# phi written as exp(min(x, 0)) + max(x, 0): two ScalarE reads of the PSUM bank, a sum on GpSimd, shared staging tiles and a new order

## The chip, the core and the metric

The kernel runs on one core of one Trainium2 chip, in one launch. The time is device microseconds of that core. The kernel before took 338.68 us as the median of three runs (338.31 to 340.45). A profiled execution of it, from which all durations below come, took 337.45 us.

## The reference

Two independent results are computed and set side by side. The first is a memory-augmented attention over 2048 positions of 448 features: 16 heads of 28 features, 4 segments of 512 positions. The second is a state-space convolution of another 2048x448 input.

```python
phi = lambda t: jnp.where(t > 0, t + 1.0, jnp.exp(t))
for s in range(N):                       # 4 segments
    qs, ks, vs = q[:, :, s], k[:, :, s], v[:, :, s]
    logits = einsum("bhqd,bhkd->bhqk", qs, ks) * scale + mask
    a_dot = einsum("bhqk,bhkd->bhqd", softmax(logits), vs)
    pq = phi(qs)
    num = einsum("bhld,bhde->bhle", pq, M)
    den = einsum("bhld,bhd->bhl", pq, z)[..., None] + 1e-6
    outs.append(g * num / den + (1.0 - g) * a_dot)
    pk = phi(ks)
    M = M + einsum("bhld,bhle->bhde", pk, vs)
    z = z + einsum("bhld->bhd", pk)
return concat(outs) @ wo                 # and, beside it, y + u * D_skip
```

For the second result the kernel has a short form, a running sum along the positions, that it uses where a bound computed on the chip allows it. For these inputs the running sum is what the chip executes; the general convolution is skipped.

## The kernel before, in words

**Tiling.** The 16 heads are taken four at a time, 32 partitions to a head (28 features, the others carry sums and the softmax maximum). A unit of work t = 4s + g is one group g of four heads in one segment s; t runs from 0 to 15. For each unit there are these stages, each a function of the kernel:

- `P_proj` (lines 470, 474, 475): q and k of the unit, 11 matmuls each into one PSUM bank; ScalarE writes the high half and VectorE the low half of each value, so that products keep float32 accuracy.
- `phi` (lines 495 to 497): phi of q or of k, from the same PSUM bank, or, for the k of group 3, from a sum of the halves in SBUF.
- `M_upd` (522, 524, 530, 538, 540): phi(k) is transposed, copied to SBUF by ScalarE, multiplied with v and added to the memory M.
- `P_num` (508, 510): phi(q) times M.
- `Q1` (558, 566): logits row block by row block in three parts. Each part fills four banks, one a head; VectorE reduces each bank to a row maximum (a custom instruction and a read of its accumulator). `Q1_max` (573 to 577) transposes the maxima and sends them by DMA into the rows of q.
- `Q2` (593, 597, 600): transposed logits with the maximum subtracted, again in three parts of four banks; ScalarE takes the exponential of each bank into P0, P1 or P2 and GpSimd blanks the upper triangle.
- `PV` (617) multiplies with v; the row sums travel by DMA (`rc`), are inverted on VectorE and spread into buffers `R` (632 to 639).
- `C_unit` (683 to 690): GpSimd multiplies by `R`, adds the two parts and takes the low half; `C_last` does the same for t = 15 mostly on VectorE, in two halves of the positions.
- `V_tile` (428, 431) makes v, `W_tile` (701, 707) the output projection, four parts (one for each group) of three matmuls to a tile.
- `B_tile` (761 to 770): a tile of the convolution; ScalarE scales into `sc`, VectorE scans (764), GpSimd carries the last column and adds (766, 769).

**PSUM.** There are eight banks, and all stages draw from the same eight (room "f"). A part of `Q1` or `Q2` takes four of them at once.

**Three tilings of the array.** `Q1` and `Q2` put the four heads in four strips of rows of the array, `PV` and the second half of `M_upd` in four strips of columns, and all other matmuls use the whole array. They are called row, column and full below.

**Order.** Every operation is first recorded in a list by `Plan.op`, with its engine and the tiles that it reads and writes. `Plan.write` then emits the operations one after the other in the order of the table ORDER. So the table alone decides where an instruction stands in the queue of its engine, and which buffer of a room it gets: the one that has been free longest at that place. Each engine works through its queue in that order; an instruction that waits for a buffer or an operand holds up all that stand behind it on its engine. SyncE issues most of the DMAs, in the order of its own queue. The priorities in AT are recorded with the operations, but do not take part in the emission.

The tiles that the change touches are declared in these lines:

```python
room("R", 2, [P, 512], F32)
room("u", 2, [112, 512], F32)
room("sc", 1, [112, 512], F32)
```

Of the kernel before, what the change touches and what calls it, by code (L numbers as in the profile page):

```python
# [8 lines left out]
F32 = mybir.dt.float32  # L9
F32R = mybir.dt.float32r  # L10
I32 = mybir.dt.int32
AF = mybir.ActivationFunctionType
# [6 lines left out]
P = 128  # L19
# [236 lines left out]
def attn_s4d_kernel(tc, xT, wq, wk, wv, wo, beta, u, uT, lar, aim, crl, cim, ldt, dsk, ldc, dsc, oa, yT):  # L256
# [5 lines left out]
    with ExitStack() as ctx:  # L262
# [23 lines left out]
        room("P1", 2, [P, 4, 384], F32)  # L286
        room("P2", 1, [P, 4, 384], F32)
        room("pvn", 2, [P, 2, 512], F32)
        room("R", 2, [P, 512], F32)
        room("oh", 5, [P, 512], F32R)  # L290
        room("ol", 5, [P, 512], F32R)
        room("u", 2, [112, 512], F32)
# [609 lines left out]
```

## Time and profile before

| | |
|---|---|
| median of three runs | 338.68 us |
| profiled execution | 337.45 us, of it the span from first to last instruction 335.5 us and 1.95 us around it |
| TensorE (PE) | 319.9 us busy, 95% of the span |
| VectorE (DVE) | 246.4 us, 73% |
| ScalarE (ACT) | 215.0 us, 64% |
| GpSimd (POOL) | 163.3 us, 49% |
| chain that ended last | PE 83%, DVE 6%, ACT 5%, DMA 3%, issue 2% |

How to read it: the busy time of PE says that it nearly always has a matmul under way, but a matmul that waits for its operands or its bank, or that runs at a lowered clock, also counts as under way. The chain is the better guide to what sets the end: it follows back, from the last instruction, to whatever released each step. The time that it gives to DVE, ACT, DMA or issue is time in which PE was held up. The row PEclk of the page, and the column PEclk of a table by stretches, give the share of the TensorE clock that was granted. In the profile, `L566` and the like are lines of the kernel; buffer numbers are left out of the names.

### The profile page before, as it was taken

The page shows a single profiled execution, that of the slowest core. Times are in us where ns is not written, and L with a number is a line of the kernel's source. Part 1 is how long each engine was busy: PE and PEld are TensorE (multiplying, and loading weights), DVE is VectorE, ACT ScalarE, POOL GpSimd, SP SyncE. Part 2 cuts the span into 40 slices and gives each one's busy share as a digit, 9 for nine tenths or more (in the row PEclk, how much of TensorE's full clock was granted, in tenths as well). Part 3 has the DMA queues.
Part 4 walks back from the last instruction along what each step waited for, and adds up shares of the span by engine and source line. Part 5 has one row for each costly group of instructions (what it writes and reads, how often), then busy time and mean ns, then how long its engine had stood idle before and what let it go on. Part 6 is the DMA issues. An engine that isn't in the chain of part 4 may idle for free.

```text
span 335.5 us, 8677 instructions
## 1 busy us (share of the span) xinstructions
PE 319.9 (95%) x3221; PEld 220.2 (66%) x3221; DVE 246.4 (73%) x777; ACT 215.0 (64%) x439; POOL 163.3 (49%) x208
## 2 busy tenths in 40 slices
PE   7999989998999999999999999899999999899992
PEld 2677866686686577677767777666666757546662
DVE  2999986798869794954899846677498868446680
ACT  4845378986794659778845865558743565757721
POOL 9035046346281628555654412587471361746920
PEclk9999989999999999999999969999999999979999
DMA  7942232211221203121022310310100131110113
GB/s 211 308 141 68 78 116 91 69 59 59 74 63 43 78 31 109 55 71 42 6 82 96 93 65 24 95 59 4 39 8 4 37 110 40 41 53 10 57 55 113
DMA packets 16584, 23.92 MB, mean 71 GB/s; under 512 B 4364, under 2 KB 9500, under 8 KB 16540
## 3 DMA queue, kind: packets, MB, share of 16 engines
q1 hardware_dynamic: 16252, 22.82, 22.0%
q10 hardware_dynamic: 288, 0.52, 0.6%
q8 instruction: 26, 0.43, 0.6%
q14 instruction: 18, 0.15, 0.2%
HBM read 13.64 MB, written 7.36 MB: 63 GB/s over the span
## 4 chain that ended last, share of the span: by engine, by line
PE 83%; DVE 6%; ACT 5%; DMA 3%; issue 2%; ACTq 0%; DVEq 0%
PE f L470 22%; PE f L558 13%; PE f L701 11%; PE f L617 11%; PE f L593 10%; PE f L428 10%; PE f L508 3%; ACT P L597 3%; DVE f L566 2%; DMA P<-in_wk 2%; PE f L522 2%; PE f L530 1%; DMA rc<-pvn 1%; PE f L573 1%; DVE mx L566 1%
## 5 line engine op out<-in xcount | busy, mean ns | idle before, releaser
L566 DVE CUSTOM_DVE_ANT_0 f<-f,mask 128x384 f32<-128x384 f32 (+3 forms) x256 | 118.0, 521 | 31.9 <-PE f L558 27.1
L597 ACT ACTIVATE P<-f 128x384 f32<-128x384 f32 (+1 forms) x192 | 89.3, 536 | 18.3 <-PE f L593 17.3
L600 POOL TENSOR_SCALAR_AFFINE_SELECT P<-P 128x512 f32<-128x512 f32 x64 | 41.5, 666 | 48.7 <-ACT P L597 48.6
L558 PE MATMUL f<-k,q 28*128 28x384 f32 (+3 forms) x768 | 51.6, 353 | 3.3 <-DMA q<-mr 1.4
L593 PE MATMUL f<-q,k 29*128 29x256 f32 (+3 forms) x768 | 48.2, 346 | 1.5 <-DVE mx L566 0.6
L683 POOL TENSOR_TENSOR pvn<-pvn,R 128x512 f32<-128x512 f32 x26 | 34.6, 1338 | 30.8 <-DVE R L639 24.7
L558 PEld LDWEIGHTS f<-k,q 28*128 28x128 f32 x768 | 32.5, 188 | 21.3 <-DVE mx L566 7.1
L593 PEld LDWEIGHTS f<-q,k 29*128 29x128 f32 x768 | 32.6, 190 | 15.8 <-ACT P L597 4.7
L617 PE MATMUL f<-P,vb 128*32 128x256 f32 (+3 forms) x528 | 39.7, 440 | 0.0
L566 DVE DVE_READ_ACCUMULATOR2_ANT mx<- 128x1 f32 x256 | 35.9, 140 | 0.1
L617 PEld LDWEIGHTS f<-P,vb 128*32 128x32 f32 x528 | 17.3, 112 | 21.3 <-issue 16.0
L690 POOL TENSOR_TENSOR ol<-pvn,oh 128x512 fp32r<-128x512 f32 x15 | 19.3, 1284 | 19.4 <-ACT oh L689 19.4
L470 PE MATMUL f<-xh,wh_q 128*128 128x512 f32 x64 | 28.3, 443 | 0.0
L701 PE MATMUL f<-wh_o,oh 128*128 128x448 f32 x64 | 26.6, 415 | 0.8 <-ACT oh L673 0.7
L764 DVE TENSOR_TENSOR_SCAN sc<-ones,carry,sc 112x512 f32<-112x512 f32 x16 | 23.0, 1435 | 5.0 <-ACT sc L762 4.9
L470 PE MATMUL f<-xh,wl_q 128*128 128x512 f32 x64 | 25.9, 405 | 0.0
L428 PE MATMUL f<-wh_v,xh 128*128 128x448 f32 x64 | 25.4, 397 | 0.0
L769 POOL TENSOR_TENSOR u<-u,sc 112x512 f32<-112x512 f32 x16 | 20.5, 1283 | 7.7 <-ACT u L767 7.7
L428 PE MATMUL f<-wl_v,xh 128*128 128x448 f32 x64 | 23.4, 365 | 0.0
L701 PE MATMUL f<-wl_o,oh 128*128 128x448 f32 x64 | 23.4, 365 | 0.0
L701 PE MATMUL f<-wh_o,ol 128*128 128x448 f32 x64 | 23.4, 365 | 0.0
L470 PE MATMUL f<-xh,wh_k 128*128 128x512 f32 x48 | 21.1, 441 | 1.9 <-ACT xin L524 1.1
(138 smaller groups left out, 568.7 us busy)
## 6 DMA issues: line engine op xcount, KB each, us to landing
u<-in_uT SPq DMA_DIRECT2D x16, 224.0 KB
out_y<-u SPq DMA_DIRECT2D x16, 224.0 KB
out_a<-os SPq DMA_DIRECT2D x16, 224.0 KB
xin<-in_xT SPq DMA_DIRECT2D x12, 256.0 KB
P<-in_xT SPq DMA_DIRECT2D x4, 256.0 KB
k<-q SPq DMA_DIRECT2D x64, 16.0 KB
P<-in_wv SPq DMA_DIRECT2D x4, 224.0 KB
xin<-in_wo SPq DMA_DIRECT2D x4, 224.0 KB
```

Source lines behind the costliest of these rows:

```text
L428: nc.tensor.matmul(pv.ap, X(s, x, c).ap[:, cs], (wl if w else wh).ap[:, c], start=a, stop=b)
L470: nc.tensor.matmul(pp.ap, (wl if w else wh).ap[:, g, c], X(s, x, c).ap, start=a, stop=b)
L558: nc.tensor.matmul(bank[h].ap[:, c0:c0 + n], q.ap[rows(h), qb, a, :], k.ap[rows(h), 0:qb + 1, b, :], start=(i == 0), stop=(i == 2))
L566: nc.vector.tensor_tensor_reduce(sc, sc, mask[:, 512 - n:512], 1.0, -3.0e38, ALU.add, ALU.max, mx.ap[:, 4 * h + qb:4 * h + qb + 1])
L593: nc.tensor.matmul(bank[h].ap[:, c0:c0 + w], k.ap[rows(h, 29), kb, a, :], q.ap[rows(h, 29), kb:4, b, :], start=(i == 0), stop=(i == 2))
L597: Q.op("ACT", act(n), pri + 0.01 * h, lambda h=h: nc.scalar.activation(pb.ap[:, h, 0:n], bank[h].ap[:, 0:n], AF.Exp, scale=SCALE), r=[bank ...
L600: Q.op("POOL", 700, pri + 0.1, lambda c0=c0: nc.gpsimd.affine_select(pb.ap[:, :, c0:c0 + P], pb.ap[:, :, c0:c0 + P], [[0, 4], [1, P]], ALU ...
L617: nc.tensor.matmul(pvp.ap[32 * h:32 * h + 32, q0:hi], VB(s, kb).ap[:, 4 * g + h, :], pb.ap[:, h, c0 + q0 - kb * P:c0 + hi - kb * P], start ...
L683: nc.gpsimd.tensor_tensor(pvn.ap[:, i, :], pvn.ap[:, i, :], R[i].ap, ALU.mult)
L701: nc.tensor.matmul(po.ap, o.ap[:, cs], w.ap[:, g], start=(g == 0 and i == 0), stop=(g == 3 and i == 2))
L764: Q.op("DVE", 1354, pri, lambda: nc.vector.tensor_tensor_scan(sc.ap, ones.to_broadcast([112, 512]), sc.ap, cj, ALU.mult, ALU.add), r=[sc, ...
L769: Q.op("POOL", 1344, pri, lambda: nc.gpsimd.tensor_tensor(ut.ap, ut.ap, sc.ap, ALU.add), r=[ut, sc], w=[ut])
```

## The change

The value of phi is split as phi(x) = exp(min(x, 0)) + max(x, 0). Before, ScalarE wrote relu(-x) into the result tile, then exp of its negative in place, and VectorE read the PSUM bank again and took max(x + 1, that). Now ScalarE reads the bank twice, for relu(-x) into the result tile and for relu(x) into a buffer of room "R", takes the exponential in place as before, and GpSimd adds the two tiles, both in SBUF. The bank has no reader on VectorE any more. phi is evaluated 24 times: for k in the units 0 to 11 and for q in the units 4 to 15.

Room "R" grows from two buffers to three, and room "sc" goes: `B_tile` now takes its 112 rows from a buffer of "R". Three users draw on "R": `phi`, the spread reciprocals of `PV`, and `B_tile`. The buffer of phi is taken when the first relu is emitted (`hold=[r]`).

The order table is replaced as a whole. Below, two of its lines and the core of the rest; the lines below `phi` move down by five numbers, so that line 558 becomes 563, 593 becomes 598, 701 becomes 706.

```diff
 ORDER = """
-5 11 6 8 12 0 9 2 90 14 3 48 17 7 15 13 10 4 30 54 22 51 24 1 45 49 18 31 79 91 16 92 19 50 108 100 109 32 25 46 26 47
+5 0 2 8 11 6 3 51 20 14 17 9 7 12 15 48 45 81 4 24 10 13 30 39 90 27 42 1 16 18 19 46 49 25 83 82 50 33 100 26 91 108
...
-        room("R", 2, [P, 512], F32)
+        room("R", 3, [P, 512], F32)
...
-        room("sc", 1, [112, 512], F32)
...
-            Q.op("ACT", act(512), pri, lambda: nc.scalar.activation(e.ap, at(), AF.Relu, scale=-1.0), r=[d], w=[e])
+            r = Q.buf("R")
+            Q.op("ACT", act(512), pri, lambda: nc.scalar.activation(e.ap, at(), AF.Relu, scale=-1.0), r=[d], w=[e], hold=[r])
+
+            def plus():
+                nc.scalar.activation(r.ap, at(), AF.Relu)
+            Q.op("ACT", act(512), pri, plus, r=[d], w=[r])
             Q.op("ACT", act(512), pri, lambda: nc.scalar.activation(e.ap, e.ap, AF.Exp, scale=-1.0), r=[e], w=[e])
-            Q.op("DVE", 800, pri, lambda: nc.vector.scalar_tensor_tensor(e.ap, at(), 1.0, e.ap, ALU.add, ALU.max), r=[d, e], w=[e])
+            Q.op("POOL", 1344, pri, lambda: nc.gpsimd.tensor_tensor(e.ap, e.ap, r.ap, ALU.add), r=[e, r], w=[e])
...
-            ut, sc = Q.buf("u"), Q.buf("sc")
+            ut, sc = Q.buf("u"), Q.buf("R", lambda z: z[0:112])
```

The new table moves work on every engine. Two places are shown, since the prediction speaks of them. The first is on TensorE, late in the program, in units 13 to 15. The rows are matmuls; `f_65` to `f_72` are the eight banks, `q_..`, `k_..` the tiles of a unit. Before, the last four matmuls of the first part of `Q1` of unit 15 (line 558) stand directly ahead of the first four of the second part of `Q2` of unit 14 (line 593):

```order
L558 MATMUL f_68<-k_91,q_89 128x256
L558 MATMUL f_66<-k_91,q_89 128x256
L558 MATMUL f_70<-k_91,q_89 128x256
L558 MATMUL f_69<-k_91,q_89 128x256
L593 MATMUL f_65<-q_88,k_90 128x384
L593 MATMUL f_72<-q_88,k_90 128x384
L593 MATMUL f_71<-q_88,k_90 128x384
L593 MATMUL f_69<-q_88,k_90 128x384
```

At the same place now (lines 563 and 598), two parts of an output tile (line 706) stand between them:

```order
L563 MATMUL f_65<-k_93,q_89 128x256
L563 MATMUL f_71<-k_93,q_89 128x256
L706 MATMUL f_69<-wh_o,oh_109 128x448
L706 MATMUL f_69<-wl_o,oh_109 128x448
L706 MATMUL f_69<-wh_o,ol_114 128x448
L706 MATMUL f_69<-wh_o,oh_110 128x448
L706 MATMUL f_69<-wl_o,oh_110 128x448
L706 MATMUL f_69<-wh_o,ol_115 128x448
L598 MATMUL f_72<-q_88,k_91 128x384
L598 MATMUL f_68<-q_88,k_91 128x384
L598 MATMUL f_71<-q_88,k_91 128x384
L598 MATMUL f_70<-q_88,k_91 128x384
```

Six matmuls of the full array have moved in between two parts that need four banks each. Right behind this place, the third part of `Q1` of unit 15 followed at once before; now the 16 column matmuls of `M_upd` of unit 10 and `PV` of unit 13 stand ahead of it.

The second place is in the queue of ScalarE, in the middle of the program, around phi of k of unit 7. `R_..` and `sc_..` are staging buffers, `u_..` a tile of the convolution, `P_..` receive exponentials. Before:

```order
L597 ACTIVATE P_103<-f_66 128x384
L762 ACTIVATE sc_120<-u_118,c0t 112x512
L474 CAST q_87<-f_69 128x4x128
L524 COPY xin_73<-f_71 128x512
L495 ACTIVATE phk_99<-xin_74 128x512
L597 ACTIVATE P_103<-f_65 128x384
L495 ACTIVATE phq_98<-f_69 128x512
L496 ACTIVATE phk_99<-phk_99 128x512
L597 ACTIVATE P_100<-f_67 128x512
```

Now:

```order
L496 ACTIVATE phq_98<-f_68 128x512
L499 ACTIVATE R_107<-f_68 128x512
L499 ACTIVATE R_108<-xin_74 128x512
L767 ACTIVATE R_106<-u_119,c0t 112x512
L496 ACTIVATE phk_99<-xin_74 128x512
L694 CAST oh_110<-pvn_105 128x512
L628 COPY pvn_104<-f_70 128x512
L474 CAST q_89<-f_66 128x4x128
L501 ACTIVATE phq_98<-phq_98 128x512
L501 ACTIVATE phk_99<-phk_99 128x512
```

Three rows in succession now write the three buffers of room "R". The last readers of `R_108` and `R_106` ahead of this are multiplications of unit 6 on GpSimd (line 688, the former 683), which stand in that engine's queue behind the multiplications, the sum and the subtraction of unit 5.

119 rows, old and new, of the table ORDER are left out of this document.

## The prediction

> **What bounds the kernel now.** I read the page first: the busy time of the engines, the clock row and the chain that ended last.
>
> ```profile
> span 335.5 us, 8677 instructions
> PE 319.9 (95%) x3221; PEld 220.2 (66%) x3221; DVE 246.4 (73%) x777; ACT 215.0 (64%) x439; POOL 163.3 (49%) x208
> PEclk9999989999999999999999969999999999979999
> PE 83%; DVE 6%; ACT 5%; DMA 3%; issue 2%; ACTq 0%; DVEq 0%
> ```
>
> TensorE bounds the kernel, but not wholly: 17% of the chain, 57 us, is not PE. The change leaves the matmuls as they are, so what it can win lies in that part. Where it lies in the middle of the program is told by the chain taken for single stretches (the line "by line" gives shares of the stretch; below it start, length and work). Four of them stand out:
>
> ```profile
> by line: PE f L470 30.6%; PE f L593 27.9%; PE f L558 14.9%; DVE f L566 13.7%; ACT P L597 9.8%; DVE mx L566 3.3%; PE f L573 1.0%; issue 0.8%
> 50.09 3.37 PE f L470 x11
> by line: PE f L593 44.5%; PE f L558 25.4%; ACT P L597 19.8%; PE f L470 9.1%; PE f L701 7.5%; issue 1.2%
> 194.47 1.96 PE f L558 x10
> 197.81 2.86 PE f L470 x6
> by line: PE f L617 31.5%; ACT P L597 16.2%; DVE f L566 15.3%; PE f L558 12.5%; PE f L701 12.0%; PE f L593 5.3%; ACT os L707 4.4%; DVE mx L566 3.5%; issue 1.7%
> 294.17 3.78 PE f L617 x32
> by line: PE f L593 47.2%; ACT P L597 28.1%; PE f L558 19.6%; PE f L522 6.4%; issue 2.6%
> ```
>
> They are the stretches 43 to 54, 190 to 198, 286 to 298 and 298 to 302 us. In each, PE waits for DVE's row maxima (L566) and ACT's exponentials (L597), which empty the banks of `Q1` and `Q2`. The same pieces of PE work undisturbed, two `W_tile` parts, the group of the exponentials, and the granted clock by stretches (the third figure from the right):
>
> ```profile
> 274.40 2.32 PE f L617 x32
> 286.28 1.45 PE f L701 x6
> L597 ACT ACTIVATE P<-f 128x384 f32<-128x384 f32 (+1 forms) x192 | 89.3, 536 | 18.3 <-PE f L593 17.3 <-POOL pvn L687 0.4 <-DVE ry L634 0.3
> 215.94 1.60 PE f L470 x6
> 71.04 2.84 PE f L470 x11
> 184.52 2.75 PE f L470 x11
> 40.00:60.00 20.00, 18.95 (x259) 13.22 (x257) 14.44 (x52) 16.63 (x37) 9.27 (x13) 0.91 0.34 103
> 180.00:200.00 20.00, 19.71 (x197) 14.71 (x196) 15.30 (x61) 14.67 (x30) 7.09 (x8) 0.87 0.28 82
> 280.00:300.00 20.00, 18.71 (x191) 11.55 (x190) 11.72 (x41) 13.23 (x29) 10.33 (x11) 0.91 0.07 21
> ```
>
> So each of the first three waits was followed by work at a lowered clock: 3.78 us instead of 2.32 at 294, 2.86 instead of 1.60 at 198. Waits and clock together: 43 to 54, 27.6% of 11 us plus 3.37 - 2.75, 3.6 us; 190 to 198, 21.0% of 8 us plus 1.26 and the stretched L558 piece (1.96, which takes some 0.9 elsewhere), 4.0 us; 286 to 298, 41.1% of 12 us plus 1.46, 6.4 us; 298 to 302, 30.7% of 4 us, 1.2 us. That is 15.2 us.
>
> **The change part by part.** The arithmetic of phi, by the grouped rows (busy, mean ns):
>
> ```profile
> L497 DVE SCALAR_TENSOR_TENSOR phq<-f,phq 128x512 f32<-128x512 f32 x12 | 8.1, 678 | 1.7 <-ACT phq L496 1.6
> L497 DVE SCALAR_TENSOR_TENSOR phk<-f,phk 128x512 f32<-128x512 f32 x9 | 6.2, 684 | 1.6 <-ACT phk L496 1.5
> L497 DVE SCALAR_TENSOR_TENSOR phk<-xin,phk 128x512 f32<-128x512 f32 x3 | 2.0, 667 | 0.0
> L495 ACT ACTIVATE phq<-f 128x512 f32<-128x512 f32 x12 | 7.1, 593 | 5.1 <-PE f L508 4.4 <-DVE q L475 0.8
> L495 ACT ACTIVATE phk<-f 128x512 f32<-128x512 f32 x9 | 5.4, 599 | 5.9 <-PE f L522 2.4 <-DVE k L475 2.2 <-PE f L470 1.2
> L495 ACT ACTIVATE phk<-xin 128x512 f32<-128x512 f32 x3 | 2.1, 686 | 0.0
> L769 POOL TENSOR_TENSOR u<-u,sc 112x512 f32<-112x512 f32 x16 | 20.5, 1283 | 7.7 <-ACT u L767 7.7
> ```
>
> It takes 8.1 + 6.2 + 2.0 = 16.3 us from DVE (246 to 230), adds the second relu at the price of the first, 7.1 + 5.4 + 2.1 = 14.6 us, to ACT (215 to 230), and 24 sums at 1.283 us, 30.8 us, to POOL (163 to 194). Each phi is ready some 1.2 us later (+0.60 + 1.28 - 0.68). That lies beside other work: its readers on PE stand several matmul groups further on in both orders. All three engines stay far below PE's 320. As to the chain, 6% of it is DVE, 20 us in 246, 5% ACT, 17 us in 215, so in proportion the two edits are worth -1.3 and +1.2 us, which I put at nothing.
>
> [...]
>
> The order matters more. *Bursts.* A third part of `Q1` or `Q2` in close succession needs banks that the first two have not given back. In the order before, the largest bursts are five such parts with little between them (at 190 to 198), four at 287 to 294, and five about 43 to 50; the first piece of the order shown above is in the second of these, and bank `f_69` is written by one part and wanted by the next. In the new order two or three parts is the most: W parts, a projection or `PV` stand between the others. A W part gives 0.7 us of cover (1.45 for two), `PV` 2.3, against some 2 us in which ACT empties four banks (four exponentials of 0.536). At 286 to 298 I take 5.5 of 6.4 us as won, at 190 to 198 3.5 of 4.0, at 43 to 54 only 1.0 of 3.6 (three `Q2` parts still follow each other), at 298 to 302 nothing (the same three parts still follow each other): -10.0 us. Its bounds are 0 and -15.2.
>
> *Changes of tiling.* The new order breaks the runs of row matmuls more often: PE passes between full and row tiling 142 times instead of 122. The price is read from the steps between starts:
>
> ```profile
> 163.62 0.39 PE L470 MATMUL f<-xh,wh_k 128*128 128x512 f32 x1
> 163.86 0.40 PE L470 MATMUL f<-xh,wl_k 128*128 128x512 f32 x1
> 164.18 1.06 PE L558 MATMUL f<-k,q 28*128 28x128 f32 x24
> 165.17 0.50 PE L470 MATMUL f<-xh,wh_q 128*128 128x512 f32 x1
> 165.51 0.39 PE L470 MATMUL f<-xh,wl_q 128*128 128x512 f32 x1
> 165.74 0.39 PE L470 MATMUL f<-xl,wh_q 128*128 128x512 f32 x1
> ```
>
> The step is 0.23 to 0.24 within the projection, 0.32 into the row matmuls and 0.34 just after them, so 0.1 us a passage: +2.0 us, all of it on PE.
>
> *Start and end.* ACT now casts the first two tiles of x ahead of the weights of k, and PE begins with q.
>
> ```profile
> 8.57 0.51 PE L470 MATMUL f<-xh,wh_k 128*128 128x512 f32 x1 [0.64 <-ACT xh L400]
> 321.54 0.47 PE L701 MATMUL f<-wh_o,oh 128*128 128x448 f32 x1 [0.73 <-ACT oh L673]
> ```
>
> Of the 0.64 us I count 0.5 as won. At the end, the wait of 0.73 us for the last high half goes, since four W parts instead of two, and the second half of `PV`, stand between it and the first half of `PV`: -0.7 us. In both places it could be nothing.
>
> *The ring of three R buffers.* Seven writes of ACT into "R" now come within 1 us of PE work behind the last reader on POOL of the same buffer; the second piece shown above is two of them. ACT would wait there, and behind it exponentials and casts for which PE waits. The nearest row is the old `sc`, a single buffer with two such places:
>
> ```profile
> L762 ACT ACTIVATE sc<-u,c0t 112x512 f32<-112x512 f32 x16 | 11.7, 729 | 1.1 <-DMA u<-in_uT 0.7 <-POOL u L769 0.4
> ```
>
> That cost 0.4 us, 0.2 a place, so 1.4 for seven; at worst each waits for a whole POOL instruction, 7 x 1.283 = 9.0. I take 3.0, nearer to the row, but above it, since POOL is fuller now.
>
> The sum: -10.0 + 0 + 2.0 - 0.5 - 0.7 + 3.0 = -6.2 us, against the profiled 337.45 (span 335.5) 331.25. The median of the runs lies 1.2 us above the profiled execution, so the forecast is 332.5 us. Less than 1% (3.4 us) either way is what a measurement of this kernel cannot tell from no change.
>
> **The rivals.** *The waits move.* The bursts may be a sign that nothing else was ready for PE; then the new order only shifts the wait. For it: ACT, which empties the banks of `Q2`, is busy 16.63 of the 20 us from 40 to 60 already and only gets more to do. Against it: at 286 W parts were ready and were spent just before the burst. If half the gain comes, -5.0 - 1.2 + 2.0 + 3.0 = -1.2: 337.5 us.
>
> *The R ring paces ACT, slower.* The place is the middle, units 5 to 9, where three R writes stand in a row in ACT's queue and from phi of k of unit 8 to phi of q of unit 9 POOL's queue holds 16 instructions of 1.28 us, 20.5 us in all. If all seven places cost a POOL instruction and half of the burst gain is lost for the same reason, -5.0 - 1.2 + 2.0 + 9.0 = +4.8: 343.5 us. It decides for slower when the seven waits average more than about 0.6 us with half the gain gone. Against it speaks the 0.4 us above.
>
> *POOL and DVE shut each other out, slower.* Two rows show what POOL can do to a short DVE instruction (min, median, max of one line):
>
> ```profile
> L633 DVE TENSOR_SCALAR rc<-rc,mix x15: 241/245/1181, 71.0 to 310.1; 128x32 f32<-128x32 f32 x15
> L633 DVE TENSOR_SCALAR rc<-rc,mix 128x32 f32<-128x32 f32 x15 | 8.9, 595 | 0.5
> ```
>
> Fifteen instructions of 0.24 us take 8.9 us, 5.3 more than their work, with POOL 49% busy. In proportion to POOL's 194 us that is one microsecond more. But if each of the 24 sums holds DVE up for its whole length, DVE gains 31 us of waiting for the 16 it is rid of, bursts stay as they are (0 of -10), and its 15 us add 1.2 on the chain: 0 - 1.2 + 2.0 + 3.0 + 1.2 = +5.0, 343.7 us. [...]
>
> **How the numbers follow.** The forecast has 0.55, the moved waits 0.25, the ring 0.15, the ports 0.05. The forecast's own range is 327.5 (13.4 us of bursts won, ring at 1.4) to 335. The range, 327.5 to 343.0, takes in the moved waits and the near half of the two slow cases. Faster by over 1% is 0.55, within 1% 0.25, slower 0.20.
>
> **What would show it.** Right: the chain's shares of DVE and ACT fall at the places of the late W tiles and of unit 8 to 10; the clock row keeps its 9 there; `PV` of unit 13 takes 2.3 us; L497's successor on POOL is about 1.28 us x24; passages of tiling cost 0.1 us. Wrong: ACT rows of the relu into R or of the convolution's scale show waits on POOL of over 5 us in all; ACT's exponentials hold PE up in units 5 to 9; new low digits in the clock row; L633 with a mean above 0.8 us.

## The result, and the profile after

The changed kernel took 327.53 us (median of four executions, 326.69 to 330.36), the kernel before 338.5 us beside it. The ratio is 0.969, with a 95% interval from 0.961 to 0.978: faster, by 11 us. Executions of the kernel before on one chip lay between 333.92 us at a granted clock of 0.989 and 339.37 us at 0.970, and the ratios and intervals leave out those more than 1.5% above the kernel's fastest. The profiled execution took 326.69 us, its span 324.6.

The page of the changed kernel, the rows that answer to the first ones shown of before (span, busy times, granted clock, chain):

```profile
span 324.6 us, 8711 instructions
PE 311.6 (96%) x3221; PEld 213.6 (66%) x3221; DVE 226.7 (70%) x753; ACT 225.3 (69%) x463; POOL 192.9 (59%) x232
PEclk9999999999999999999999999999999999999999
PE 70%; DVE 9%; DMA 7%; ACT 5%; POOL 3%; issue 3%; SPq 2%; ACTq 0%; DVEq 0%
```

DVE lost 19.7 us of work, ACT gained 10.3 and POOL 29.6. The clock row has no low digit left; before it had three. The shares of the chain tell little: PE fell from 83% to 70%, although TensorE waits less, probably since the chain steps aside into engines that were only just on time.

Three of the four stretches that the prediction named. First two as parts of the changed kernel's chain, from 40 to 54 us and, for units 8 to 10, from 186 to 196 us (the line "by line" gives shares of the stretch), then a table by stretches whose third figure from the right is the granted clock:

```profile
by line: PE f L598 28.7%; PE f L470 21.1%; PE f L428 17.4%; PE f L622 14.7%; PE f L563 11.7%; PE f L535 5.5%; PE f L578 1.5%
by line: PE f L706 26.2%; PE f L622 23.1%; PE f L598 11.2%; PE f L513 10.6%; PE f L563 9.6%; PE f L535 7.0%; DVE f L571 6.7%; issue 4.1%; DVE mx L571 2.1%; DVEq L571 0.1%
```

And the table:

```profile
40.00:60.00 20.00, 20.00 (x260) 13.68 (x259) 13.43 (x47) 17.04 (x38) 9.48 (x10) 1.00 0.36 104
180.00:200.00 20.00, 19.32 (x280) 13.06 (x279) 14.60 (x61) 13.72 (x30) 8.59 (x11) 1.00 0.22 67
280.00:300.00 20.00, 18.87 (x278) 12.28 (x277) 11.34 (x46) 13.10 (x29) 15.19 (x16) 1.00 0.13 40
```

From 40 to 54 us the chain is PE alone, where from 43 to 54 us 17% of it had been DVE and 10% ACT. From 186 to 196 us 13% of it is not PE. What is left late in the program is seen in TensorE's own timeline (start, length, what, and in brackets the idle time before it with what ended it):

```profile
283.93 2.38 PE L622 MATMUL f<-P,vb 128*32 128x512 f32 x32
286.24 0.97 PE L563 MATMUL f<-k,q 28*128 28x512 f32 x12
287.04 0.73 PE L598 MATMUL f<-q,k 29*128 29x256 f32 x3
288.57 0.90 PE L598 MATMUL f<-q,k 29*128 29x256 f32 x21 [0.81 <-DVE mx L571]
```

`PV` of unit 13 takes 2.4 us where it had taken 3.8, with a granted clock of 0.50 up to 297.1 us. (Q2.2 is short for the third part of `Q2`, counted from 0.) Behind `PV` and Q1.2 of unit 15, Q2.2 of unit 14 still stops: its fourth matmul starts 1.5 us after its first, since its fourth bank comes from a row maximum of the part just ahead.

I counted the losses of TensorE in one more way: each group of matmuls is given its undisturbed length (the shortest that the trace of before has for its shape, with 0.1 us for each passage of tiling), and what the next group starts later than that is a stall; a lowered clock counts too. By this count the stalls are 25.9 us before and 12.6 after, and the matmuls with their passages 292.5 and 294.1. The count is an estimate of mine that no view prints: with the groups cut in another way it falls by some 11 us instead of 13.3, so take single figures as good to 2 or 3 us. In the stretch from 40 to 60 us they fall from 3.8 to 0.0, from 180 to 200 from 4.6 to 0.7, from 280 to 300 from 6.7 to 3.4.

### The profile page after: what moved, and what is told of

It is laid out like the page before. It is cut to its first block, busy times and chain, and to the rows that moved or that the text cites. A ratio compares the mean times of both kernels' runs of the same rounds, so it can differ in the third digit from the quotient of the medians.

```text
span 324.6 us, 8711 instructions
## 1 busy us (share of the span) xinstructions
PE 311.6 (96%) x3221; PEld 213.6 (66%) x3221; DVE 226.7 (70%) x753; ACT 225.3 (69%) x463; POOL 192.9 (59%) x232
## 4 chain that ended last, share of the span: by engine, by line
PE 70%; DVE 9%; DMA 7%; ACT 5%; POOL 3%; issue 3%; SPq 2%; ACTq 0%; DVEq 0%
PE f L470 18%; PE f L563 10%; PE f L428 10%; PE f L598 10%; PE f L622 8%; PE f L706 8%; DVE f L571 4%; ACT P L602 3%; PE f L513 3%; DMA P<-in_wk 2%; DMA u<-in_crl 2%; PE f L527 2%; DMA xin<-in_xT 1%; DVE mx L571 1%; PE f L535 1%
## 5 line engine op out<-in xcount | busy, mean ns | idle before, releaser
L571 DVE CUSTOM_DVE_ANT_0 f<-f,mask 128x512 f32<-128x512 f32 (+3 forms) x256 | 117.8, 520 | 38.0 <-PE f L563 33.5
L602 ACT ACTIVATE P<-f 128x384 f32<-128x384 f32 (+1 forms) x192 | 88.4, 542 | 18.3 <-PE f L598 17.5
L598 PE MATMUL f<-q,k 29*128 29x512 f32 (+3 forms) x768 | 45.3, 340 | 2.5 <-DVE mx L571 0.8
L563 PE MATMUL f<-k,q 28*128 28x512 f32 (+3 forms) x768 | 46.5, 345 | 0.8 <-DVE mx L571 0.3
L598 PEld LDWEIGHTS f<-q,k 29*128 29x128 f32 x768 | 30.4, 183 | 17.3 <-ACT P L602 4.7
L563 PEld LDWEIGHTS f<-k,q 28*128 28x128 f32 x768 | 29.8, 184 | 18.0 <-DVE mx L571 4.6
L622 PE MATMUL f<-P,vb 128*32 128x256 f32 (+3 forms) x528 | 38.0, 427 | 1.0 <-DVE mx L571 0.7
L774 POOL TENSOR_TENSOR u<-u,R 112x512 f32<-112x512 f32 x16 | 20.7, 1301 | 21.1 <-ACT P L602 9.8
L769 DVE TENSOR_TENSOR_SCAN R<-ones,carry,R 112x512 f32<-112x512 f32 x16 | 21.7, 1354 | 5.3 <-ACT R L767 5.2
L403 POOL TENSOR_TENSOR xl<-xin,xh 128x512 fp32r<-128x512 f32 x9 | 11.6, 1290 | 15.5 <-ACT xh L400 15.5
```

The source lines that it names most:

```text
L563: nc.tensor.matmul(bank[h].ap[:, c0:c0 + n], q.ap[rows(h), qb, a, :], k.ap[rows(h), 0:qb + 1, b, :], start=(i == 0), stop=(i == 2))
L571: nc.vector.tensor_tensor_reduce(sc, sc, mask[:, 512 - n:512], 1.0, -3.0e38, ALU.add, ALU.max, mx.ap[:, 4 * h + qb:4 * h + qb + 1])
L598: nc.tensor.matmul(bank[h].ap[:, c0:c0 + w], k.ap[rows(h, 29), kb, a, :], q.ap[rows(h, 29), kb:4, b, :], start=(i == 0), stop=(i == 2))
L602: Q.op("ACT", act(n), pri + 0.01 * h, lambda h=h: nc.scalar.activation(pb.ap[:, h, 0:n], bank[h].ap[:, 0:n], AF.Exp, scale=SCALE), r=[bank ...
L622: nc.tensor.matmul(pvp.ap[32 * h:32 * h + 32, q0:hi], VB(s, kb).ap[:, 4 * g + h, :], pb.ap[:, h, c0 + q0 - kb * P:c0 + hi - kb * P], start ...
L769: Q.op("DVE", 1354, pri, lambda: nc.vector.tensor_tensor_scan(sc.ap, ones.to_broadcast([112, 512]), sc.ap, cj, ALU.mult, ALU.add), r=[sc, ...
```

## The experiments

Medians, ratios to the kernel before on the same chip with 95% intervals, and the stalls of TensorE in the profiled execution by the count above:

| kernel | median us | ratio | stalls us |
|---|---|---|---|
| before (338.5 beside the changed kernel; 337.1, 336.1 and 336.5 beside the experiments) | 338.5 | 1 | 25.9 |
| changed: new order, new phi | 327.53 | 0.969 (0.961 to 0.978) | 12.6 |
| old order, new phi | 342.72 | 1.016 (1.007 to 1.026) | 33.2 |
| the same, second relu over 64 columns | 339.24 | 1.009 (1.005 to 1.012) | 28.7 |
| new order, old phi, exponential early | 350.53 | 1.040 (1.030 to 1.050) | 35.7 |
| new order, old phi, in place | 356.19 | no interval | 39.5 |
| new order, new phi, sums on VectorE | 337.35 | 1.005 (1.001 to 1.009) | 22.1 |
| new order, second relu over 64 columns | 326.09 | 0.969 (0.964 to 0.975) | 11.4 |
| old, late burst broken | 338.72 | 1.004 (1.000 to 1.008) | 24.3 |
| old, late and middle burst broken | 339.57 | 1.008 (1.002 to 1.014) | 28.1 |
| old, late order of the new one on PE | 344.65 | 1.025 (1.018 to 1.032) | 34.1 |
| new, late burst put back | 332.87 | 0.992 (0.989 to 0.996) | 20.2 |
| new, four R buffers | 326.41 | 0.970 (0.966 to 0.974) | 11.9 |
| new, late places changed | 329.57 | 0.980 (0.975 to 0.984) | 16.3 |

The changed kernel and its variants come from different sets of runs. A difference of two medians below can therefore be off by 2 or 3 us: by the ratios the sums on VectorE cost 12 us and the burst put back 8 us, where the medians say 9.8 and 5.3. Differences below that size say nothing.

### The order or the arithmetic

My theory was that the new order gives the gain and that the arithmetic cancels. The rival: the relief of VectorE gives it. The first two runs take one half of the change each.

```diff
 # against the changed kernel
-        room("R", 3, [P, 512], F32)
+        room("R", 4, [P, 512], F32)
-        room("xh", 8, [P, 512], F32R)
+        room("xh", 7, [P, 512], F32R)
 # ORDER: that of before; the second relu stands just ahead of each
 # exponential, the sum where VectorE's old instruction stood
```

> The order of before with the arithmetic of after: each phi as two ScalarE reads of the bank and a sum on GpSimd, the second relu just ahead of the exponential, the sum at the place of VectorE's old instruction; four shared staging buffers instead of three (seven tiles of x instead of eight make room), so that no ring holds it up. If the gain of 11 us comes from the order (my theory; the two edits of the arithmetic cancel), about 338.5 us, 0.995 to 1.005 of before, with the three windows of lowered clock still there. If it comes from the arithmetic (VectorE rid of 16 us, the bank free without it), 327 to 331 us, 0.97 to 0.98.

342.72 us, 1.6% above the kernel before on the same chip (337.08): neither theory. The new phi alone makes the old order slower. VectorE's busy time falls by 10.5 us here (246.4 to 235.9). Four rows of its chain, from 273 us on (start, length, what):

```profile
273.48 0.49 ACT R L499
273.97 0.51 ACT phq L501
274.47 0.50 ACT P L602
275.02 1.78 PE f L563 x11
```

And the one wait of TensorE for a sum, from the list of its waits (us in total, times, longest):

```profile
PE f L527 <- POOL phk L502: 0.8, 1, 0.8
```

In this piece of the chain the second relu stands in ScalarE's queue ahead of an exponential of `Q2` whose bank TensorE wants for `Q1` (of the chain's rows the first delays the third, the third the fourth), and the transposition of phi(k) now waits for a sum that GpSimd ends later.

```diff
 # against the kernel before; ORDER: the new one without the second relus
-        room("R", 2, [P, 512], F32)
-        room("sc", 1, [112, 512], F32)
+        room("R", 3, [P, 512], F32)
-            ut, sc = Q.buf("u"), Q.buf("sc")
+            ut, sc = Q.buf("u"), Q.buf("R", lambda z: z[0:112])
```

> The order of after with the arithmetic of before: no second relu and no sum on GpSimd; the exponential and VectorE's old instruction stand where the later of the two relus stood, so that the bank is free at the same place; three shared staging buffers for the convolution and the reciprocals. Order theory: 327 to 330 us, 0.965 to 0.975 of before. Arithmetic theory: 336 to 340 us, at most 0.995. A gain of about half would say that the order needs the lighter VectorE.

350.53 us, ratio 1.040. That run had moved the exponential of most phis forward, so I made it again with the order left in place as far as the banks allow. Counted through the table, the new order with the old phi would need ten banks at once, even with VectorE's instruction right behind the exponential, and there are eight: with the old phi a bank is held until VectorE has read it after the exponential, and the new order puts up to 72 operations of all engines between the relus and the exponential.

```diff
 # against the run above, ORDER only: the exponential at its place of
 # the new order, VectorE's old instruction where the sum stood, both
 # earlier only where a part would find no free bank
```

> The new order with the old phi once more, now with the order left as it is: the exponential stays at its place in all but three of the 24 phis, VectorE's old instruction stands where the sum stood on GpSimd, and it comes earlier only where a part would otherwise find no free bank. The bank of a phi is held until that instruction, not until the second relu. If the order alone gives the gain, 327 to 331 us, 0.97 to 0.98. If the new order needs the bank given back early, as the first two runs suggest (1.016 for the new phi in the old order, 1.040 for the old phi in the new one), 337 us or more, at least 1.0.

356.19 us (350.49 to 358.55 in four executions, without an interval; even the fastest is 4% above the kernel before). So neither half can do without the other: 1.016 with the new phi alone, 1.040 and more with the new order alone, 0.969 with both. A part of it shows in what the weight loads of `Q1` and `Q2` wait for, because the wait for a bank stands there. First this kernel, then the changed one (us in total, times, longest):

```profile
PEld f L557 <- DVE mx L565: 11.0, 24, 1.6
PEld f L592 <- DVE mx L565: 6.9, 17, 1.2
```

```profile
PEld f L563 <- DVE mx L571: 4.6, 13, 0.8
PEld f L598 <- DVE mx L571: 4.3, 9, 1.1
```

17.9 us of waiting for row maxima against 8.9 with the same order on TensorE. The kernel before has 9.5 of it (7.1 and 2.4), so this sum tells the two kernels of the new order apart, not the changed kernel from the one before.

### VectorE, ScalarE and the place of the sum

```diff
 # against the changed kernel
-            Q.op("POOL", 1344, pri, lambda: nc.gpsimd.tensor_tensor(e.ap, e.ap, r.ap, ALU.add), r=[e, r], w=[e])
+            Q.op("DVE", 800, pri, lambda: nc.vector.tensor_tensor(e.ap, e.ap, r.ap, ALU.add), r=[e, r], w=[e])
```

> The changed kernel with one edit: the 24 sums run on VectorE instead of GpSimd, at the same place of the order, so that ScalarE's queue is as in the changed kernel, GpSimd has 31 us less and VectorE some 16 us more. If where the sum runs does not matter (arithmetic at nothing, as predicted), 326.5 to 329 us, 0.968 to 0.975 of before. If the gain is VectorE's relief, 331 to 335 us, 0.98 to 0.99. If GpSimd's queue costs the changed kernel something, 1 to 2 us below it.

337.35 us, 9.8 us above the changed kernel, and beyond what I had given the rival (331 to 335). The order is the same on every other engine, and the banks come free at the same instruction. So the new order with banks given back early is not enough either: without VectorE's relief its ratio is 1.005, and the whole gain is gone. The page of this kernel (busy times, clock, chain):

```profile
PE 318.0 (95%) x3221; PEld 215.8 (64%) x3221; DVE 245.4 (73%) x777; ACT 225.4 (67%) x463; POOL 168.2 (50%) x208
PEclk9999999999999999999999999999999999999998
PE 56%; DVE 24%; DMA 6%; ACT 5%; issue 4%; POOL 3%; SPq 1%; DVEq 0%; POOLq 0%; ACTq 0%
```

Its sums (min, median, max in ns):

```profile
L502 DVE TENSOR_TENSOR phk<-phk,R x12: 647/690/1574, 19.0 to 262.6; 128x512 f32<-128x512 f32 x12
L502 DVE TENSOR_TENSOR phq<-phq,R x12: 650/688/1676, 71.1 to 308.5; 128x512 f32<-128x512 f32 x12
```

A piece of its chain late in the program:

```profile
290.24 1.62 DVE phq L502
```

And what its weight loads wait for, to be held against the 4.3 and 4.6 of the changed kernel above:

```profile
PEld f L598 <- DVE mx L571: 7.2, 15, 1.2
PEld f L563 <- DVE mx L571: 6.4, 19, 0.8
```

VectorE has 18.7 us more work than in the changed kernel (245.4 against 226.7), the span is 10.1 us longer: half of it lies on the path, at an undisturbed clock. VectorE is busy no more than 73% of the time, but its row maxima give back the banks of `Q1`, and what stands between them in its queue delays the next part. One sum of 1.62 us is on the chain by itself. In the timelines of GpSimd and VectorE it stands so:

```profile
290.04 1.27 POOL L688 TENSOR_TENSOR pvn<-pvn,R 128x512 f32<-128x512 f32 x1
290.18 1.68 DVE L502 TENSOR_TENSOR phq<-phq,R 128x512 f32<-128x512 f32 x1
```

Six of the 24 sums take over 1 us, 4.5 us above the median in all, and each of the six starts while a TENSOR_TENSOR of GpSimd is running. So the 9.8 us are the price of these sums beside a busy GpSimd; what the same work would cost beside an idle GpSimd was not tried.

```diff
 # against the run "old order, new phi"
-                nc.scalar.activation(r.ap, at(), AF.Relu)
+                nc.scalar.activation(r.ap[:, 0:64], at()[:, 0:64], AF.Relu)
 ...
 # the sum reads the 64 columns eight times
```

> The first run once more (order of before, arithmetic of after, 342.7 us, 1.016 of before), with the second relu taken over 64 of its 512 columns; the sum on GpSimd reads these 64 eight times, so its work and its waits stay, but phi is not computed rightly for x > 0. VectorE keeps its relief of 16 us, ScalarE has only some 6 us more than before instead of 15. If the second relu on ScalarE is what the old order cannot take, 334 us or less, below 0.99. If it is the later sum on GpSimd, or a new order is needed to use VectorE's relief, 340 us or more, at least 1.007.

339.24 us: 3.5 us of the excess of that run (2.5 by the ratios) go with 8.4 us of ScalarE's work (225.4 to 217.0). The rest stays. So in the old order the second relu costs, and VectorE's relief brings nothing that shows; the sum that comes later, or the old places of the row maxima, stand against it, and which of the two was not tried.

```diff
 # the same edit of the relu and the sum, against the changed kernel
```

> The changed kernel with the second relu taken over 64 of 512 columns, as in the run above (phi not computed rightly for x > 0); order, buffers and waits as they are. It takes some 8 us from ScalarE. If ScalarE's work is off the path of the new order, as the prediction put it (1.2 us for the whole 14.6), 326 to 328 us, 0.966 to 0.973. If ScalarE paces it, 320 to 323 us, 0.95 to 0.957.

326.09 us, 1.4 us below the changed kernel's median, with intervals that overlap, for 8.1 us less on ScalarE. In the new order ScalarE's work costs little: at most 1.4 us for 8.1, where the prediction had 1.2 for 14.6.

### The bursts

```diff
 # against the kernel before, TensorE in units 13 to 15 (nothing else moves
 # but the copy behind W2.2); Wa.b gN is part N of tile b of segment a
  Q2.2 t13
- W2.2 g1
  Q2.1 t13
- W2.2 g2
- W2.2 g3
+ W2.2 g1
  Q2.0 t13
  Q1.0 t15
+ W2.2 g2
+ W2.2 g3
  Q2.1 t14
+ PV t13
  Q1.2 t15
- PV t13
  Q2.2 t14
```

> Before, with only the late burst broken up, by matmul groups that were there anyway: of the W parts of tile 2 of segment 2 one moves between the third and the first part of Q2 of unit 13, two between Q1.0 of unit 15 and Q2.1 of unit 14, and PV of unit 13 moves ahead of Q1.2 of unit 15. Nothing else changes. Burst theory: of the 6.4 us of waits and lowered clock from 286 to 298 us 5.5 go, 333 us, 0.984 of before (0.980 to 0.988), and the low digit of the clock at 290 to 298 us goes too. If the waits only move to the next place, 336 to 338.5 us, 0.993 to 1.0.

338.72 us, ratio 1.004: nothing won. (The first W part ends up between Q2.1 and Q2.0 of unit 13, as the diff has it.) TensorE's timeline shows where the waits went:

```profile
285.29 1.10 PE L558 MATMUL f<-k,q 28*128 28x128 f32 x24 [0.95 <-DMA k<-q]
...
292.01 0.29 PE L593 MATMUL f<-q,k 29*128 29x256 f32 x2
293.16 0.38 PE L593 MATMUL f<-q,k 29*128 29x256 f32 x1 [0.85 <-DVE mx L566]
```

Q1.0 of unit 15 now comes early enough to wait for the rows of k that travel by DMA, and Q2.2 of unit 14 stands where Q1.2 of unit 15 had stood and waits for its maxima. The three W parts are the same three; put into one gap they leave another. This is the rival "the waits move".

```diff
 # against the run above, TensorE in units 8 to 10
- W1.3 g0, g1, g2, g3
  Q2.0 t8
  Q1.0 t10
  Q1_max t9
+ W1.3 g0, g1, g2, g3
  Q2.1 t8
  Q1.2 t10
  Q2.2 t8
```

> The kernel with the late burst broken, and in the middle of the program the four W parts of tile 3 of segment 1 moved from ahead of the five parts of Q1 and Q2 (at 190 us) to behind the second of them. The last three parts still stand close. Burst theory: 2 to 3 us more than the late burst alone, 330 to 331.5 us, 0.976 to 0.981 of before, and one low digit of the clock more goes. If the waits move, no more than 1 us below the other.

339.57 us, ratio 1.008. By the count of stalls, 180 to 200 us has 5.3 us of them instead of 4.6 before.

Was it the cover that was missing? The next run gives the kernel before TensorE's order of the changed kernel in units 13 to 15, where the W parts are not spent on the wait for the maxima of unit 13.

```diff
 # against the kernel before, TensorE (25 groups), the others with the least shift
- Q1_max t14, prq t15, P_num t13, Q1_max t13, W2.1 g0, g1, W2.2 g0, W2.1 g2, g3, Q2.2 t13, ...
+ Q1_max t14, Q1_max t13, W2.1 g0, P_num t13, prq t15, W2.1 g1, Q2.2 t13, W2.1 g2, Q2.1 t13, W2.1 g3, Q2.0 t13, ...
```

> The kernel before, old phi, with TensorE's order of units 13 to 15 taken from the changed kernel for 25 matmul groups: the maxima of unit 13 go out before the projection of unit 15 instead of after it, so that no W part is spent on waiting for them, and the eight W parts of tiles 1 and 2 lie one or two at a time between the parts of Q2 and Q1. The other engines follow with the least shift. The late burst alone brought nothing, since it took the W parts from places that needed them. If it is this cover that was missing, 4 to 6 us less than before, 332 to 334 us, 0.98 to 0.988. If the place is bound by ScalarE or VectorE whatever PE does, 0.995 to 1.01.

344.65 us, ratio 1.025, the opposite. Its chain from 276.9 to 280.6 us; between the first and the last of these rows it shows only the row maxima on VectorE and short gaps, of which one is given:

```profile
276.90 0.94 PE f L558 x20
...
279.31 0.32 DVE f L566
...
280.60 0.27 PE f L573
```

`Q1_max` of unit 13 stands earlier on TensorE, but VectorE reaches the row maxima of that unit no earlier; TensorE waits 2.7 us for them. So this order on TensorE does not help by itself; it needs the maxima earlier, and those are VectorE's order and load.

The last run of this group goes the other way and puts the burst back into the changed kernel.

```diff
 # against the changed kernel, TensorE in units 13 to 15
  W2.1 g1
+ W2.1 g2
  Q2.2 t13
- W2.1 g2
+ W2.2 g0
+ W2.1 g3
+ W2.2 g1
  Q2.1 t13
- W2.1 g3
+ W2.2 g2
+ W2.2 g3
  Q2.0 t13
- W2.2 g0
- W2.2 g1
  Q1.0 t15
- W2.2 g2
- W2.2 g3
  Q2.1 t14
+ Q1.2 t15
  M_upd t10
  PV t13
- Q1.2 t15
  Q2.2 t14
```

> The changed kernel with the late burst put back: the eight W parts of tiles 1 and 2 of segment 2 come early, as before, and Q2.0 of unit 13, Q1.0 of unit 15, Q2.1 of unit 14 and Q1.2 of unit 15 follow each other with nothing between, PV of unit 13 behind them. If bursts cost what the prediction took, 3 to 6 us more than the changed kernel, 330.5 to 333.5 us, 0.977 to 0.987 of before, with a low digit of the clock at 285 to 300 us in most executions. If the waits only move, 327 to 329 us, 0.968 to 0.974.

332.87 us, 5.3 us above the changed kernel; all ten executions lie between 332.37 and 334.11. TensorE alone is shown in the diff; some places on ScalarE and VectorE follow it. The waits at the end of the burst, and the granted clock (third figure from the right) in three stretches of 3.4 us around it:

```profile
286.45 1.73 PE L563 MATMUL f<-k,q 28*128 28x512 f32 x11 [0.28 <-DVE mx L571]
289.14 0.66 PE L535 MATMUL f<-vb,xin 128*32 128x32 f32 x32 [0.96 <-DVE mx L571]
```

```profile
283.90:287.30 3.40, 2.76 (x28) 1.57 (x25) 2.11 (x12) 1.94 (x6) 3.40 (x4) 1.00 0.00 0
287.30:290.70 3.40, 2.11 (x45) 0.91 (x41) 2.37 (x9) 1.43 (x4) 2.59 (x4) 0.51 0.01 2
290.70:294.10 3.40, 3.40 (x28) 1.28 (x24) 1.55 (x8) 0.00 (x0) 0.61 (x2) 0.50 0.03 5
```

So the late burst, with the places that follow it, costs about what the prediction took, 5.5 us, where the other engines let its removal be used. The clock falls with it: half from 287 to 294 us.

### The ring, and an attempt at more

```diff
 # against the changed kernel
-        room("R", 3, [P, 512], F32)
+        room("R", 4, [P, 512], F32)
-        room("xh", 8, [P, 512], F32R)
+        room("xh", 7, [P, 512], F32R)
```

> The changed kernel with four buffers in room R instead of three (seven tiles of x instead of eight make room). If the ring costs the 3 us of the prediction, 323.5 to 325.5 us, 0.957 to 0.965. By the waits in the changed kernel's profile (1.1 us before the second relu, 0.6 before the convolution's scale, most of it not on the chain) it is 0 to 1 us, 326.5 to 328 us, 0.967 to 0.972.

326.41 us, 1.1 us below the changed kernel's median, and not to be told from it (0.970, 0.966 to 0.974).

```diff
 # against the changed kernel, TensorE and ScalarE in units 13 to 15
  PV t13
+ P_num t14
  Q1.2 t15
  Q2.2 t14
- P_num t14
  Q2.0 t14
 # ScalarE: one exponential of Q2.1 t14 ahead of the high half of C_unit t12,
 # the first relu of phi(q) t15 behind the copy of PV t13
```

> An attempt at a faster version: the changed kernel with the two waits that are left at 287 to 293 us attacked. P_num of unit 14 moves ahead of Q1.2 of unit 15 on TensorE; on ScalarE the first relu of phi of q of unit 15 then comes some 4 us earlier and gives its bank back for Q2.2 of unit 14, and one exponential moves ahead of a high half that waits for GpSimd. If the late waits end on banks, 1 to 2 us less than the changed kernel, 325.5 to 327 us, 0.963 to 0.969. If they only move to Q2.0 and Q1.1 behind, 327 to 329 us.

329.57 us: 2 us above the changed kernel's median (3.7 by the ratios). The stop in Q2.2 of unit 14 that it was to end is still there:

```profile
287.76 0.34 PE L598 MATMUL f<-q,k 29*128 29x256 f32 x3
289.30 1.16 PE L598 MATMUL f<-q,k 29*128 29x256 f32 x22 [1.20 <-DVE mx L571]
```

The fourth matmul starts 1.5 us after the first, as in the changed kernel (1.54 and 1.53; the idle time in brackets is longer only because the three matmuls ahead take 0.34 instead of 0.73). `P_num` ahead of Q1.2 makes that part 0.7 us later, and its maxima with it; what stands behind then has no cover. Its executions also have a lower granted clock (0.985 to 0.991) than three of the changed kernel's four (0.996 to 0.999).

## Why the prediction was right, and where it was not

The time came out at 327.53 us against the forecast of 332.5, on the side that had the greatest chance, but only just inside the range from 327.5 to 343.0. The gain was too small by 5 us in the sum, and the sum gives it to the wrong part: all of it to the order, nothing to the arithmetic. That the time still came near is in part luck, since the change holds both; the order alone, by the runs, loses 4%.

- **Bursts, -10.0.** The size was about right: by the count of stalls 11.0 us went in the three stretches (13.3 in the whole kernel, start, end and ring included). At 43 to 54 us I had taken 1.0 of 3.6 because three parts of Q2 still follow each other; by the count all of it went. At 180 to 200 us it was as forecast for 190 to 198 (3.9 for 3.5). Late, 3.3 us of stalls went from 280 to 300, and the last run of that group prices the burst itself at 5.3 (forecast 5.5). What is left there is a burst that the prediction missed when it said that two or three parts is the most: Q1.2 of unit 15, Q2.2 and Q2.0 of unit 14 and Q1.1 of unit 15 stand in a row in the new order, with only `P_num` of unit 14 among them, and the 0.81 us shown above lie in it. The cause as I put it, a few parts in a row without cover, is not enough: the same cover moved within the old order won nothing (1.004 and 1.008), and TensorE's new late order on the old engines lost 2.5%.
- **Arithmetic, nothing in the chain.** This is the step that failed. "In proportion the two edits are worth -1.3 and +1.2 us": in the new order the sums away from VectorE are worth 9.8 us, seven times that; the second relu is worth at most 1.4 for the part taken away, near the forecast. In the old order the new phi costs 1.6%, and 3.5 us of it are the second relu. The share of an engine in the chain is an average over stages, and VectorE's work seems worth most where its row maxima give back banks: the waits for them rise from 8.9 to 13.6 us when VectorE takes the sums. It also depends on what the order makes of it, so that no single price per microsecond holds.
- **The two terms are not to be added.** The order is what it is because a bank is free after the second relu, without the exponential and without VectorE. With the old phi it has too few banks and loses 4% or more. The prediction treated an arithmetic edit of small price and an order of large price; the runs show one change that works only whole.
- **Tiling passages, +2.0.** The count of stalls cannot test it, since it takes the 0.1 us a passage as given. The price itself is seen in the changed kernel too, 0.23 us from start to start within a projection, 0.32 into the row matmuls:

```profile
17.65 0.39 PE L470 MATMUL f<-xh,wh_q 128*128 128x512 f32 x1
17.88 0.39 PE L470 MATMUL f<-xh,wl_q 128*128 128x512 f32 x1
18.20 0.97 PE L563 MATMUL f<-k,q 28*128 28x128 f32 x24
```

- **Start, -0.5.** The row matmuls behind the first block of q and k begin at 15.29 us instead of 15.71, but three groups on the same place is reached at 19.10 instead of 18.98. Nothing was won.
- **End, -0.7.** The wait of 0.73 us for the last high half is gone from the list of TensorE's waits; what stands there now (us in total, times, longest) leaves about 0.5 won:

```profile
PE f L706 <- DVE ol L679: 0.2, 1, 0.2
```

- **R ring, +3.0.** Mis-sized. The waits before the writes are small, 0.4 us of them for the multiplications on GpSimd that I had feared, 0.6 for the one in the last unit, and a fourth buffer wins about 1 us at most:

```profile
L499 ACT ACTIVATE R<-f 128x512 f32<-128x512 f32 x21 | 12.7, 606 | 1.1 <-POOL pvn L688 0.4 <-DVE q L475 0.3 <-DVE k L475 0.2
L767 ACT ACTIVATE R<-u,c0t 112x512 f32<-112x512 f32 x16 | 11.6, 728 | 0.6 <-POOL pvn L668 0.6
L502 POOL TENSOR_TENSOR phk<-phk,R 128x512 f32<-128x512 f32 x12 | 15.5, 1292 | 4.1 <-ACT phk L501 3.3 <-ACT R L499 0.8
L502 POOL TENSOR_TENSOR phq<-phq,R 128x512 f32<-128x512 f32 x12 | 15.5, 1291 | 4.4 <-ACT phq L501 4.3
```

The sums on GpSimd take 1.29 us each, as forecast.

The rivals. *The waits move* happened in the changed kernel only in small part (the stop in Q2.2 of unit 14), but in three of the experiments (both with broken bursts, and the attempt at more) it is all that happened. I found no way to tell these apart in the profile of before. *The R ring* fell with the rows above. *POOL and DVE shut each other out* (the ports, 0.05): in the changed kernel the short instruction that showed it got better, not worse (min, median, max):

```profile
L638 DVE TENSOR_SCALAR rc<-rc,mix x15: 241/242/691, 58.3 to 301.1; 128x32 f32<-128x32 f32 x15
```

And the group of the row maxima (busy, mean ns, idle before):

```profile
L571 DVE CUSTOM_DVE_ANT_0 f<-f,mask 128x512 f32<-128x512 f32 (+3 forms) x256 | 117.8, 520 | 38.0 <-PE f L563 33.5 <-ACT P L602 2.7 <-ACT phk L501 1.4
```

Its maximum fell from 1.18 to 0.69 us, and the row maxima keep their 520 ns (521 before) beside 30 us more of GpSimd. The wait itself is in the trace of before: seven of the 15 short instructions start while a TENSOR_TENSOR of GpSimd is running, take 0.42 to 1.18 us and end 0.03 to 0.13 us after it; the other eight take 0.24 to 0.25. The longest:

```profile
211.96 1.28 POOL L403 TENSOR_TENSOR xl<-xin,xh 128x512 fp32r<-128x512 f32 x1
212.10 1.18 DVE L633 TENSOR_SCALAR rc<-rc,mix 128x32 f32<-128x32 f32 x1
```

Where VectorE takes the sums, six of 24 are long, up to 1.68 us with a median of 0.69, and each of the six starts behind a running GpSimd instruction. That each sum on GpSimd holds VectorE up for its whole length is not shown: the changed kernel's row maxima, 0.73 us at the longest in both kernels, show no sign of it.

The clock. Of the list of what would show it, the chain's shares were a poor sign (ACT's fell at units 8 to 10, DVE's rose), and the clock row was a good one: it kept its 9 in the profiled execution (one of the other three, at 330.36 us, had a mean clock of 0.981). Beside the experiments the kernel before ran 50 times that are compared here, with a granted clock from 0.964 to 0.990 and times from 333.45 to 338.45 us; a line through them falls by 1.8 us for each 0.01, with a scatter of 0.8. The changed kernel ran at 0.981 to 0.999. Drawn on to 0.997 the line gives 332.9 us for the kernel before. So some 5.4 us of the gain would stand at an equal clock, and the rest, 3.4 us from the median of these 50 executions (336.3) or 5.6 from the 338.5 beside the changed kernel, goes with the higher clock. It is an estimate, since no execution of before had that clock, and the line does not part what the clock costs from what the waits cost beside it.

## What to carry to other kernels

An order written for one set of instructions is fitted to it: price an arithmetic edit and a new order together; here either one alone lost. Work on an engine that empties PSUM banks can cost far more than its share of the chain (here VectorE's did, 9.8 us for 18.7 us of work, where its share gave 1.3 for 16.3; ScalarE's in the new order did not, at most 1.4 us for 8.1); ask what stands in its queue between two evictions that TensorE wants. Before moving cover from one gap to another, count it: three matmul groups that already hide a wait can only hide another in its place.

## What the runs showed of the hardware

In the profiled executions of before and of the changed kernel the granted clock is 1.00 or 0.50. Ahead of its last microsecond the kernel before has three stretches at half, of 3.41, 6.83 and 3.41 us; the changed kernel has none from 6.8 to 324.2 us. The three (the third figure from the right is the granted clock):

```profile
47.97:51.38 3.41, 3.41 (x24) 2.56 (x21) 3.11 (x14) 2.79 (x7) 2.92 (x4) 0.50 0.67 199
194.74:201.57 6.83, 6.83 (x53) 5.13 (x52) 2.25 (x8) 3.91 (x10) 1.71 (x3) 0.50 0.11 38
293.73:297.14 3.41, 3.41 (x26) 0.85 (x24) 2.70 (x8) 1.10 (x3) 3.19 (x4) 0.50 0.00 0
```

The granted clock of before in two stretches of 3.4 us, late in the program, and in one in the middle, and of the changed kernel in two around its last long wait:

```profile
290.30:293.70 3.40, 2.75 (x24) 1.57 (x23) 2.63 (x16) 2.02 (x5) 2.92 (x4) 1.00 0.03 5
293.70:297.10 3.40, 3.40 (x24) 0.81 (x22) 2.70 (x8) 1.13 (x3) 3.21 (x4) 0.50 0.00 0
211.81:215.22 3.41, 2.02 (x17) 1.59 (x20) 2.95 (x5) 1.97 (x5) 3.05 (x4) 1.00 0.45 121
```

```profile
286.70:290.10 3.40, 2.58 (x38) 1.50 (x30) 2.36 (x7) 1.26 (x4) 1.63 (x2) 1.00 0.44 122
290.10:293.50 3.40, 3.22 (x28) 2.08 (x27) 2.91 (x10) 3.38 (x8) 1.84 (x2) 1.00 0.06 20
```

Ahead of the last of the three half stretches TensorE has 2.75 us busy of 3.40, and the longest wait in TensorE's list of before is 1.5 us. But such a stretch does not foretell a lower clock: the changed kernel has one with 2.58 us busy of 3.40 and kept its clock, and the kernel before kept it behind the one with 2.02 of 3.41 at 212 us, so something not seen here decides too.

VectorE's sum of two tiles in SBUF takes 0.65 us at the least and up to 1.68 us beside a busy GpSimd, while its reductions that read and write PSUM keep 520 ns in the same run (521 before). I had not expected that the same 24 sums cost the kernel 10 us more on one engine than on the other.
